# Pooled attention and a gated MLP on one core: float32 probabilities and values in the first two query groups, part of the first weight decode through SBUF, a new order

## The chip, the core and the metric

The kernel runs on one core of a Trainium2 chip. TensorE (PE) multiplies matrices out of SBUF into PSUM. VectorE (DVE), ScalarE (ACT) and GpSimd (POOL) work elementwise; POOL reads and writes SBUF alone. SyncE (SP) issues transfers, and so does ACT in this kernel. Each engine takes its instructions in the order in which the program has them. The metric is the device time of one execution in microseconds; lower is better.

## The reference, cut to what matters

Queries are pooled by two, attended over 1152 keys, and each token's 8 heads of 64 go through a normalized, gated MLP. The weights of the MLP arrive as float64, the rest as float32.

```python
def _attn_ref(q, k, v):                       # 4 batches, 8 heads, 1152 rows, 64 columns
    q_pool = q.reshape(B, H, S // factor, factor, D).mean(axis=3)
    scores = scale * np.matmul(q_pool, k.transpose(0, 1, 3, 2))
    scores = scores - np.max(scores, axis=-1, keepdims=True)
    attn = np.exp(scores)
    attn = attn / (np.sum(attn, axis=-1, keepdims=True) + 1e-09)
    return np.matmul(attn, v).astype(np.float32)

def _moe_ref(x, w_gate, w_val, w_out, rms_g):  # 2304 tokens, 512 wide, 1536 hidden
    rms = np.sqrt(np.mean(x * x, axis=-1, keepdims=True) + 1e-06)
    xn = x / rms * rms_g
    g = xn @ w_gate
    silu = g * (1.0 / (1.0 + np.exp(-g)))
    val = xn @ w_val
    return (silu * val @ w_out).astype(np.float32)
```

## The kernel before

**Precision.** PE multiplies float16 throughout. Where one float16 is too coarse, a float32 value is kept as a high and a low half: `hi_of` (L304 on ACT, L306 on DVE) casts it to float16, `lo_of` (L311, L313) takes what the cast lost. A product of two such values is made of three of the four combinations (`TERMS`); low times low is left out.

**Attention.** Each batch has 576 pooled queries: two full groups of 256 and a rest of 64. A full group has eight strips, one for each head, of 256 queries; the rest has four strips of two heads. In all 12 groups and 80 strips; the first two groups, of batch 0, are strips 1 to 16. For a group, PE first multiplies queries and keys for the row maxima alone (L699), and DVE reduces them (L708), 24 reductions for a full group; the maxima are put into the low half of the queries. Then, for a strip, `emit_scores` (L766) makes the transposed scores with the maximum already taken off, in three PSUM tiles of 768 columns, `emit_exp` (L784) takes the exponential on ACT, `emit_cast` makes the high half of the probabilities (`pT`, L304 or L306), and `emit_lo` the low half: on POOL (L311) if the exponential was put into a scratch tile `p` in SBUF (pool `p32`), on DVE if it was left in PSUM. `emit_pv` (L808) multiplies probabilities and values: for each of two halves of the queries and nine blocks of keys a matmul of the high half with low and high values (130 columns) and one of the low half with the high values (65 columns), 36 in a strip, into the one PSUM bank `o`. `emit_na` (L826) adds the two parts of the result with a reduction on DVE and so frees `o`. The 65th column of the values is a constant, and gives the sum of the probabilities.

**Values and keys.** A head's values are loaded into `st` (ACT queue) and split into high and low halves in one of eight tiles `vv` (L304 or L306, then L313 on DVE). Batch 0's keys are split and turned by PE at the start (L541), those of later batches by a transposing transfer.

**Normalization and MLP.** When a group is done, `add_norm` divides by the sums, normalizes, splits and turns the tokens (`xts`). `add_mlp` multiplies them with gate and value weights (L1011), 48 matmuls of 256 columns to a PSUM tile `ps`, then takes tanh on ACT (L1029), two steps on DVE (L1032, L1035), a cast and a remainder into `hh`, and multiplies with the output weights (L1058).

**Weights.** Float64 words are decoded in 24 jobs of one or two pieces of 512 columns (12 for gate and value, 12 for the output weights): ACT rounds the low words (L390), DVE shifts the high words into a PSUM tile (L395) and joins them (L399), POOL adds both (L405), then cast and remainder as above. All of it is in `add_w`.

**Order.** Every step is an entry in a planner (`Plan`): which engines can do it and for how long by the planner's own tables, what it needs, which buffers it takes and frees, and a rank. `Plan.run` draws up the time line of all engines from that and picks at each point the step that can start first, by rank where there are several. The `T_` constants at the head of the kernel shift the ranks. The program is then written out in that order, and no engine departs from it. PSUM has three tiles `ps` (for maxima, scores, gate and value sums, and the weight decode), `acc` and `o`.

## Time and profile before

| | |
|---|---|
| median of 3 runs | 894.13 us (893.48 to 896.4) |
| span of the profiled execution | 894.0 us (the page gives no other time of it) |
| PE busy | 814.3 us (91%), 8432 matmuls |
| DVE busy | 582.2 us (65%) |
| ACT busy | 528.1 us (59%) |
| POOL busy | 460.3 us (51%) |
| chain that ended last | PE 76%, DVE 10%, ACT 6%, DMA 4% |

The busy time of PE is modelled from pipelined matmuls: a busy PE is not PE at its peak, so the work of a stretch is better read from the count of its matmuls and the spacing of matmuls that run without gaps. The shares are means over stages with different limits. A wait is put down to the step that ended last before it. The granted clock in the table by stretch is that of PE as a share of 2.4 GHz; half of it is 1.2 GHz.

### The profile page before, as it was taken

To read this page: it belongs to the slowest core of one execution; us is meant where nothing else is said; L and a number is where in the kernel's file an instruction comes from. 1 tells how busy PE (TensorE), PEld (TensorE's weight loads), DVE (VectorE), ACT (ScalarE), POOL (GpSimd) and SP (SyncE) were. 2 spreads that over 40 slices of the span, in tenths; PEclk is the share of its full clock that TensorE was granted. 3 is DMA by queue.
4 is the path that set the end of the run, shared out by engine and by line. 5 is a ranking of instruction groups with operands and counts; after the bars stand their busy time and mean duration, and the time that the engine had idled before them with its cause. 6 is when DMAs were issued, how large, how long until landed. Compare 5 with 4: busy or idle time off the path is not lost.

```text
span 894.0 us, 20286 instructions
## 1 busy us (share of the span) xinstructions
PE 814.3 (91%) x8432; PEld 626.6 (70%) x8432; DVE 582.2 (65%) x805; ACT 528.1 (59%) x780; POOL 460.3 (51%) x403
## 2 busy tenths in 40 slices
...
GB/s 315 142 139 143 173 101 163 65 129 184 172 148 86 99 54 94 45 152 162 172 88 51 48 69 63 160 161 118 48 32 69 81 49 34 9 48 1 25 1 24
DMA packets 126956, 87.57 MB, mean 98 GB/s; under 512 B 87184, under 2 KB 105616, under 8 KB 126864
## 3 DMA queue, kind: packets, MB, share of 16 engines
...
## 4 chain that ended last, share of the span: by engine, by line
PE 76%; DVE 10%; ACT 6%; DMA 4%; issue 3%; ACTq 1%; POOL 1%; SPq 0%; POOLq 0%; DVEq 0%
PE ps L1011 30%; PE acc L1058 15%; PE ps L766 14%; PE o L808 11%; PE ps L699 6%; ACT p L784 3%; DVE mx L708 3%; DMA kh<-kT 1%; DVE wg L313 1%; DVE ps L395 1%; DVE vv L313 1%; DMA qT<-q 1%; DMA kT<-kk 1%; DVE wo L399 1%; ACT pT L304 1%
## 5 line engine op out<-in xcount | busy, mean ns | idle before, releaser
L311 POOL TENSOR_TENSOR pT<-p,pT 128x768 f16<-128x768 f32 (+1 forms) x202 | 335.4, 1681 | 123.0 <-DVE pT L306 62.7
L1011 PE MATMUL ps<-xts,wg 128*128 128x256 f16 x2592 | 307.2, 274 | 7.1 <-DVE p L1035 2.9
L1011 PEld LDWEIGHTS <-wg 128*128 128x128 f16 x2592 | 251.7, 98 | 49.4 <-issue 10.8
L708 DVE TENSOR_REDUCE mx<-ps 128x2 f32<-128x768 f32 x216 | 201.3, 953 | 35.0 <-PE ps L699 32.9
L784 ACT ACTIVATE p<-ps,lnp 128x768 f32<-128x768 f32 (+1 forms) x202 | 171.7, 874 | 61.8 <-PE ps L766 50.9
L766 PE MATMUL ps<-qT,kT 128*128 128x256 f16 (+1 forms) x864 | 162.4, 251 | 18.0 <-ACT p L784 12.3
L766 PE MATMUL ps<-qT,kh 65*128 65x256 f16 (+1 forms) x864 | 162.7, 252 | 7.3 <-DMA qT<-q 4.6
L1058 PE MATMUL acc<-wo,hh 128*128 128x512 f16 x648 | 152.5, 379 | 0.8 <-ACT p L1071 0.7
L808 PE MATMUL o<-vv,pT 128*128 128x130 f16 (+2 forms) x2880 | 141.6, 212 | 10.9 <-DVE x L826 6.5
L808 PEld LDWEIGHTS <-pT 128*128 128x128 f16 (+1 forms) x2880 | 132.7, 103 | 24.8 <-POOL pT L311 10.6
L304 ACT ACTIVATE pT<-p 128x768 f16<-128x768 f32 (+1 forms) x167 | 134.8, 824 | 2.7 <-DVE sm L915 0.8
L699 PE MATMUL ps<-kT,qT 128*128 128x384 f16 (+1 forms) x480 | 108.7, 345 | 13.1 <-DVE mx L708 5.5
L1058 PEld LDWEIGHTS <-hh 128*128 128x128 f16 x648 | 62.0, 98 | 65.9 <-issue 2.2
L766 PEld LDWEIGHTS <-kh 65*128 65x128 f16 x864 | 76.7, 100 | 42.0 <-issue 26.8
L766 PEld LDWEIGHTS <-kT 128*128 128x128 f16 x864 | 77.6, 100 | 16.8 <-DVE wo L399 2.5
L1032 DVE SCALAR_TENSOR_TENSOR p<-p,ps 128x512 f32<-128x512 f32 x54 | 36.9, 684 | 77.1 <-ACT p L1029 76.6
L1029 ACT ACTIVATE p<-ps 128x512 f32<-128x512 f32 x54 | 32.2, 596 | 91.2 <-PE ps L1011 91.1
L826 DVE TENSOR_REDUCE x<-o 128x130 f32<-128x260 f32 (+1 forms) x80 | 31.7, 396 | 66.5 <-PE o L808 66.2
L699 PEld LDWEIGHTS <-qT 128*128 128x128 f16 (+1 forms) x480 | 40.8, 104 | 41.1 <-issue 24.1
L304 ACT ACTIVATE hh<-p 128x512 f16<-128x512 f32 x48 | 30.1, 628 | 49.2 <-DVE p L1035 49.2
L405 POOL TENSOR_TENSOR wo<-wo 128x1024 int32<-128x1024 int32 (+1 forms) x20 | 32.2, 1610 | 27.9 <-DVE wo L399 12.4
L1071 ACT ACTIVATE p<-acc 128x512 f32<-128x512 f32 x18 | 10.8, 597 | 56.6 <-PE acc L1058 50.4
...
## 6 DMA issues: line engine op xcount, KB each, us to landing
...
st<-in_v_dram ACTq DMA_DIRECT2D x32, 288.0 KB, 3.5
...
st<-in_k_dram ACTq DMA_DIRECT2D x24, 288.0 KB, 3.3
...
```

What stands on the lines that cost most here:

```text
L304: nc.scalar.activation(out=dst, in_=src, func=AF.Copy, scale=s)
L311: eng.tensor_tensor(out=dst, in0=src, in1=hi, op=ALU.subtract)
L405: nc.gpsimd.tensor_tensor(out=hi, in0=hi, in1=lo, op=ALU.add)
L699: nc.tensor.matmul(out=buf("ps", key)[k * n:(k + 1) * n, a * 512:a * 512 + XP], lhsT=buf("qT", (g["i"], e))[:, 0, hl, c["ci"] * n:(c["ci"] ...
L708: nc.vector.tensor_reduce(out=buf("mx", c["g"]["i"])[:, c["ci"], s:s + 2, p], in_=buf("ps", key).rearrange("p (a c) -> p a c", a=2)[:, :, ...
L766: nc.tensor.matmul(out=sT[:, o:o + n], lhsT=lhsT, rhs=qT[:, 0, hl, :n] if r == 0 else qT[:D + 1, 1, hl, :n], start=(r == 0), stop=(r == 1),)
L784: nc.scalar.activation(out=full(), in_=sT, func=AF.Exp, scale=s_scale, bias=lnp[:, 0:1],)
L808: nc.tensor.matmul(out=o[x * n:(x + 1) * n, c0:], lhsT=pT[:, a, q0:q0 + n], rhs=buf("vv", (u["b"], h))[:, j, c0:OW], start=(j == 0 and a = ...
L1011: nc.tensor.matmul(out=dst, lhsT=wg16[:, e, kb, fg, a, fo:fo + 128], rhs=rhs, start=(i == 0), stop=(i == len(XW) - 1),)
L1029: nc.scalar.activation(out=tv(), in_=gv()[:, :, 0], func=AF.Tanh, scale=0.5 / (X_S * W_S))
L1032: nc.vector.scalar_tensor_tensor(out=tv(), in0=tv(), scalar=1.0, in1=gv()[:, :, 0], op0=ALU.add, op1=ALU.mult)
L1058: nc.tensor.matmul(out=po, lhsT=hh[:, a, f, xo + t0:xo + t0 + 128], rhs=wo16[:, f, r, :], start=(f == fs[0] and a == 0 and r == 0), stop=( ...
```

## The change

In strips 1 to 16 (groups with `whole`) the exponential goes straight from PSUM to SBUF as float32, into the bytes of the two halves of `pT`; the cast and the remainder are gone, and PSUM is free after the exponential. The values of batch 0 are loaded once more, as float32 straight into a `vv` tile, with rows of 65 words (`v_whole`); `emit_pv` then makes 18 float32 matmuls of 65 columns in a strip instead of 36 float16 ones. `emit_na` becomes a copy, on ACT or DVE. The split values of batch 0 are still made, later, for the four strips of its third group, in the same tiles, with eight more small fills on POOL (L623). The scale of the sums follows (`V_ONE`, `g["vs"]`). The first seven weight jobs shift their high words into scratch tiles in SBUF (pool `p32`) instead of PSUM, in pieces of 512 columns. The planner's durations and its `T_` constants are new, and with them the order of all engines.

```diff
--- before.py
+++ after.py
...
+V_ONE = 2.0 ** -7
...
-    T_PE_M = 913.6
+    T_PE_M = 824.5
...
+    T_WHOLE = 0.2
+    T_WM_FROM = 0
+    T_WM_TO = 7
...
+    T_N_WHOLE = 2
+    N_WHOLE = T_N_WHOLE
...
@@ -389,6 +396,24 @@
         lo, _ = w_words(i)
         nc.scalar.activation(out=lo, in_=lo.bitcast(U32), func=AF.Copy, scale=2.0 ** -29)
 
+    def w_tmp(i, e):
+        return buf("p32", ("d", i, e))[:, :WP].bitcast(I32)
+
+    def w_dec_m(i):
+        _, hi = w_words(i)
+        for e in range(w_n[i] // WP):
+            nc.vector.tensor_scalar(
+                out=w_tmp(i, e), in0=hi[:, e], scalar1=3, scalar2=0x3FFFFFF8,
+                op0=ALU.logical_shift_left, op1=ALU.bitwise_and,
+            )
+
+    def w_dec_b(i):
+        _, hi = w_words(i)
+        for e in range(w_n[i] // WP):
+            nc.vector.scalar_tensor_tensor(
+                out=hi[:, e], in0=hi[:, e], scalar=-0x40000000, in1=w_tmp(i, e), op0=ALU.bitwise_and, op1=ALU.bitwise_or
+            )
+
     def w_dec_a(i):
         _, hi = w_words(i)
...
@@ -426,12 +451,17 @@
         if wjobs[i][0] == 2:
             own = [w_done[x] for x in range(i) if w_pools[x] == f"ws{wjobs[i][2]}"]
         if w_is_64:
-            r = add(f"wr{i}", "ACT", 0.25 + 0.833e-3 * n, [d], prio, lambda: w_dec_r(i))
-            a = add(f"wa{i}", "DVE", 0.3 + 2.1e-3 * n, [d], prio, lambda: w_dec_a(i),
-                    alloc=[("ps", ("w", i)), ("pa", ("w", i))], free=[("ps", ("w", i)), ("pa", ("w", i))])
-            s = add(f"ws{i}", "POOL", 0.1 + 2.13e-3 * n, [r, a], prio, lambda: w_dec_s(i))
+            r = add(f"wr{i}", "ACT", 0.19 + 0.928e-3 * n, [d], prio, lambda: w_dec_r(i))
+            if T_WM_FROM <= i < T_WM_TO:
+                tmp = [("p32", ("d", i, e)) for e in range(n // WP)]
+                b = add(f"wm{i}", "DVE", (0.15 + 0.53e-3 * WP) * n / WP, [d], prio, lambda: w_dec_m(i), alloc=tmp, port=True)
+                a = add(f"wa{i}", "DVE", (0.16 + 1.04e-3 * WP) * n / WP, [b], prio, lambda: w_dec_b(i), free=tmp, port=True)
+            else:
+                a = add(f"wa{i}", "DVE", 0.3 + 2.1e-3 * n, [d], prio, lambda: w_dec_a(i),
+                        alloc=[("ps", ("w", i)), ("pa", ("w", i))], free=[("ps", ("w", i)), ("pa", ("w", i))])
+            s = add(f"ws{i}", "POOL", 0.19 + 1.665e-3 * n, [r, a], prio, lambda: w_dec_s(i))
         h = add(f"wh{i}", t_far(n), 0, [s, g_op] + own, prio, lambda: w_hi(i))
-        w_done.append(add(f"wl{i}", {"DVE": 0.45 + 1.04e-3 * n}, 0, [h], prio, lambda: w_lo(i), free=take, port=True))
+        w_done.append(add(f"wl{i}", {"DVE": 0.18 + 1.06e-3 * n}, 0, [h], prio, lambda: w_lo(i), free=take, port=True))
 
 
...
@@ -442,6 +472,8 @@
 
     def add_group(b, i0, n, m):
         g = dict(b=b, i=len(groups), chunks=[], n=n, strips=[])
+        g["whole"] = g["i"] < N_WHOLE and n == 128
+        g["vs"] = 1.0 / V_ONE if g["whole"] else V_S
         groups.append(g)
         for x in range(m):
...
@@ -499,7 +531,11 @@
         nc.scalar.dma_start(out=dst, in_=src[b, h].rearrange("(p c) d -> p c d", c=KC))
 
     kv_op = {}
+    w_op = {}
     k_first = []
+
+    def v_whole(x):
+        return buf("vv", (*x, "w")).rearrange("p c t -> p (c t)").bitcast(F32).rearrange("p (c t) -> p c t", t=XH)
 
     def late_dma():
...
@@ -579,9 +615,16 @@
                               lambda cs=cs: buf("kT", x)[:, cs[0]:cs[-1] + 1], alloc=[] if p else [("kT", x)])
             k_first.append((kl2, ko[0]))
             return
+        if kind == "w":
+            w_op[x] = add(f"vld{x}w", "ACT", 1.3, late_dma() + [v_fill], prio, lambda: ld_kv(x, v, v_whole(x)[:, :, :D]),
+                          alloc=[("vv", (*x, "w"))], lat=0.95, hold=0.45)
+            return
+        zero = v_fill if x[0] or not N_WHOLE else add(f"vz{x}", "POOL", 0.2, [v_fill], prio,
+                   lambda: nc.gpsimd.memset(buf("vv", x)[:, :, D:XH], 0.0), alloc=[("vv", x)])
         vl = add(f"vld{x}", "ACT", 1.1, late_dma(), prio, lambda: ld_kv(x, v, buf("st", ("v", x))), alloc=[("st", ("v", x))], lat=0.95, hold=0.45)
-        vh = add(f"vh{x}", t_hi(KC * D), 0, [vl, v_fill], prio,
-                 lambda: hi_of(buf("vv", x)[:, :, XH:XH + D], buf("st", ("v", x)), V_S), alloc=[("vv", x)])
+        vh = add(f"vh{x}", t_hi(KC * D), 0, [vl, zero], prio,
+                 lambda: hi_of(buf("vv", x)[:, :, XH:XH + D], buf("st", ("v", x)), V_S),
+                 alloc=[("vv", x)] if zero is v_fill else [])
         ko[1] = add(f"vl{x}", {"DVE": 0.25 + 1.04e-3 * KC * D}, 0, [vh], prio,
                     lambda: lo_of(buf("vv", x)[:, :, :D], buf("st", ("v", x)), buf("vv", x)[:, :, XH:XH + D], V_S),
...
@@ -779,6 +822,9 @@
 
 
 
+    def p_whole(u):
+        return buf("pT", u["i"]).rearrange("p a c t -> p (a c t)").bitcast(F32)
+
     def emit_exp(u, js, key, full):
         sT = buf("ps", key)[:, :p_cols(u, js)]
...
@@ -800,6 +846,16 @@
         o = buf("o", u["i"])[:, k * OW:(k + 1) * OW]
         hs = u["heads"]
         n = 128 // len(hs)
+        if u["g"]["whole"]:
+            for j in range(KC):
+                nc.tensor.matmul(
+                    out=o[:, :XH],
+                    lhsT=p_whole(u)[:, j * w + k * 128:j * w + (k + 1) * 128],
+                    rhs=v_whole((u["b"], hs[0]))[:, j],
+                    start=(j == 0),
+                    stop=(j == KC - 1),
+                )
+            return
         for j in range(KC):
             for a in range(2):
...
@@ -822,13 +878,18 @@
         return buf("o", u["i"])[:, :m * OW].rearrange("p (m d) -> p m d", d=OW)
 
     def emit_na(u):
+        if u["g"]["whole"]:
+            hi_of(x_of(u), o_of(u)[:, :, :XH], 1.0)
+            return
         o = o_of(u).rearrange("p m (g c) -> p m c g", g=2)
         nc.vector.tensor_reduce(out=x_of(u), in_=o, op=ALU.add, axis=AX.X)
 
-    k_last, v_last, q_last = {}, {}, {}
...
+                banks = [("ps", key), ("pa", key)]
+                full = lambda j=j: p_whole(u)[:, j[0] * u["w"]:(j[-1] + 1) * u["w"]]
+                e = add(f"E{i}.{t}", "ACT", t_act(n), [s] + ([("after", c0)] if c0 else [x for x, _ in k_first] if i < 2 else []),
+                        R_E + r, lambda j=j, key=key, full=full: emit_exp(u, j, key, full),
+                        alloc=[("pT", i)] if c0 is None else [], free=banks)
+                c0 = c0 or e
+                los.append(e)
+                continue
             e = add(f"E{i}.{t}", "ACT", t_act(n), [s], R_E + r, None)
-            c = add(f"C{i}.{t}", {"ACT": 0.17 + 0.833e-3 * n}, 0, [e] + ([("after", c0)] if c0 else [x for x, _ in k_first] if i < 2 else []), R_L + r,
+            c = add(f"C{i}.{t}", {"ACT": 0.2 + 0.833e-3 * n}, 0, [e] + ([("after", c0)] if c0 else [x for x, _ in k_first] if i < 2 else []), R_L + r,
                     None, alloc=[("pT", i)] if c0 is None else [], port=True)
             c0 = c0 or c
-            lo = add(f"L{i}.{t}", {"DVE": 0.15 + 1.04e-3 * n, "POOL": 0.13 + 2.1e-3 * n}, 0, [c], R_L + r, None)
+            lo = add(f"L{i}.{t}", {"DVE": 0.15 + 1.04e-3 * n, "POOL": 0.18 + 1.914e-3 * n}, 0, [c], R_L + r, None)
...
 
             e.path, e.lo = path, lo
-            prev = s
         m = u["w"] // 128
+        whole = g["whole"]
         for k in range(m):
             last = k == m - 1
-            pv = add(f"V{i}.{k}", "PE", KC * (t_pe(OW) + t_pe(D + 1)) * (1 if len(kvs) == 1 else 1.5),
-                     los + [pv_prev[0]] + [kv_op[x][1] for x in kvs], PE_V + r, lambda k=k: emit_pv(u, k),
+            pv = add(f"V{i}.{k}", "PE", KC * T_WHOLE if whole else KC * (t_pe(OW) + t_pe(D + 1)) * (1 if len(kvs) == 1 else 1.5),
+                     los + [pv_prev[0]] + [w_op[x] if whole else kv_op[x][1] for x in kvs], PE_V + r, lambda k=k: emit_pv(u, k),
                      alloc=[("o", i)] if k == 0 else [],
-                     free=([("pT", i)] + [("vv", x) for x in kvs if k_last[x] == i]) if last else [])
+                     free=([("pT", i)] + ([("vv", (*x, "w")) for x in kvs if x_whole[x] == i] if whole
+                                          else [("vv", x) for x in kvs if k_last[x] == i])) if last else [])
             pv_prev[0] = ("after", pv)
         lead = [("after", g["strips"][0]["x"])] if u["slot"] else q_first if g["i"] < 2 else []
-        u["x"] = add(f"na.{i}", "DVE", 0.15 + 2.08e-3 * m * XH, [pv] + lead, R_N + r, lambda: emit_na(u),
+        way = {"DVE": 0.15 + 2.08e-3 * m * XH}
+        if whole:
+            way = {"ACT": 0.25 + 0.833e-3 * m * XH, "DVE": 0.15 + 1.04e-3 * m * XH}
+        u["x"] = add(f"na.{i}", way, 0, [pv] + lead, T_R_NW + r if whole else R_N + r, lambda: emit_na(u),
                      alloc=[("x", g["i"])] if u["slot"] == 0 else [], free=[("o", i)])
...
@@ -1113,8 +1188,7 @@
 
     def fill_v():
         for x in bufs["vv"]:
-            nc.gpsimd.memset(x[:, :, D:XH], 0.0)
-            nc.gpsimd.memset(x[:, :, XH + D:], 1.0)
+            nc.gpsimd.memset(x.rearrange("p c t -> p (c t)").bitcast(F32).rearrange("p (c t) -> p c t", t=XH)[:, :, D:], V_ONE)
 
...
@@ -1125,13 +1199,17 @@
     kh_fill = add("fk", "POOL", 0.6, [], -9e5, fill_k)
     v_fill = add("fv", "POOL", 0.6, [], -8e5, fill_v)
     g_op = add("g", "SP", 0.1, [], -5.0, g_load, lat=2.0, hold=0.45)
-    jobs = []
+    jobs, split = [], set()
     seen = set()
     for u in strips:
         for h in u["heads"]:
             if (u["b"], h) not in seen:
                 seen.add((u["b"], h))
                 jobs.append((u["r"] - K_AHEAD - (0 if u["b"] else T_K0), 1, "k", (u["b"], h)))
+                if u["g"]["whole"]:
+                    jobs.append((u["r"] - V_AHEAD, 2, "w", (u["b"], h)))
+            if not u["g"]["whole"] and (u["b"], h) not in split:
+                split.add((u["b"], h))
                 jobs.append((u["r"] - V_AHEAD, 2, "v", (u["b"], h)))
     for g in groups:
         for c in g["chunks"]:
```

Three places in the new order. First PE in the first strips, where a strip's product of probabilities and values begins behind scores of the next (`kT`, `kh` are keys, `vv` values, `pT` probabilities, `ps` and `o` PSUM tiles). Before:

```order
L766 LDWEIGHTS kh_74
L766 MATMUL ps_99<-qT_86,kh_74 128x256
L808 LDWEIGHTS pT_93
L808 MATMUL o<-vv_75,pT_93 128x130
L808 LDWEIGHTS pT_93
L808 MATMUL o<-vv_75,pT_93 128x65
```

and now:

```order
L809 LDWEIGHTS kh_74
L809 MATMUL ps_101<-qT_87,kh_74 128x256
L851 MATMUL o<-vv_75,pT_93 128x65 x9
L809 LDWEIGHTS kT_66
L809 MATMUL ps_100<-qT_87,kT_66 128x256
```

A pair of loads and a pair of matmuls, nine times over for each half of the queries, has become nine float32 matmuls; their weight loads are no instructions of their own in the program.

Second ACT at strips 1 and 2 (`p` is scratch, `mx` the maxima, `wo` and `wg` weights, `x` the result of attention, `lnp` a constant). Before:

```order
L784 ACTIVATE p_90<-ps_99,lnp 128x768
L304 ACTIVATE pT_94<-p_90 128x768
L390 ACTIVATE wo_105<-wo_105 128x512
L784 ACTIVATE p_91<-ps_99,lnp 128x768
L304 ACTIVATE pT_94<-p_91 128x768
L390 ACTIVATE wo_105<-wo_105 128x512
L784 ACTIVATE p_92<-ps_101,lnp 128x768
L304 ACTIVATE pT_94<-p_92 128x768
L784 ACTIVATE p_88<-ps_99,lnp 128x768
L304 ACTIVATE p_89<-mx_95 128x4
L304 ACTIVATE pT_93<-p_88 128x768
L304 ACTIVATE wg_104<-wo_105,g_sb 128x2x512
```

and now:

```order
L311 ACTIVATE q_84<-qst_83 128x512
L830 ACTIVATE pT_93<-ps_101,lnp 128x768
L830 ACTIVATE pT_93<-ps_99,lnp 128x768
L830 ACTIVATE pT_93<-ps_101,lnp 128x768
L397 ACTIVATE wo_105<-wo_105 128x512
L830 ACTIVATE pT_94<-ps_99,lnp 128x768
L397 ACTIVATE wo_105<-wo_105 128x512
L311 ACTIVATE wg_104<-wo_105,g_sb 128x2x512
L830 ACTIVATE pT_94<-ps_101,lnp 128x768
L830 ACTIVATE pT_94<-ps_100,lnp 128x768
L311 ACTIVATE wo_105<-wo_105 128x512
L311 ACTIVATE x_97<-o 128x2x65
```

Each exponential had a cast behind it; now three exponentials follow each other with weight steps between the strips, and the result's copy is in this queue. On POOL, where 43 rows into the program the remainders of `pT` began, the first one now stands 74 rows in, behind strip 16; before it stand the adds of the weight decode.

Third DVE ahead of the first row maximum (`vv` values, `wo` the staged words and `wg` gate and value weights, `kT` keys). Before:

```order
L313 SCALAR_TENSOR_TENSOR vv_75<-st_61,vv_75 128x9x64
L313 SCALAR_TENSOR_TENSOR vv_76<-st_62,vv_76 128x9x64
L395 TENSOR_SCALAR ps_100<-wo_105 128x1024
L399 SCALAR_TENSOR_TENSOR wo_105<-wo_105,ps_100 128x1024
L395 TENSOR_SCALAR ps_101<-wo_105 128x1024
L399 SCALAR_TENSOR_TENSOR wo_105<-wo_105,ps_101 128x1024
L708 TENSOR_REDUCE mx_95<-ps_99 128x2
L708 TENSOR_REDUCE mx_95<-ps_101 128x2
L313 SCALAR_TENSOR_TENSOR vv_77<-st_61,vv_77 128x9x64
```

and now:

```order
L413 SCALAR_TENSOR_TENSOR wo_105<-wo_105,p_90 128x512
L413 SCALAR_TENSOR_TENSOR wo_105<-wo_105,p_91 128x512
L313 TENSOR_SCALAR kT_72<-ps_101 128x768
L313 TENSOR_SCALAR wg_104<-wo_105,g_sb 128x2x512
L405 TENSOR_SCALAR p_92<-wo_105 128x512
L405 TENSOR_SCALAR p_90<-wo_105 128x512
L320 SCALAR_TENSOR_TENSOR wg_104<-wo_105,g_sb,wg_104 128x2x512
L413 SCALAR_TENSOR_TENSOR wo_105<-wo_105,p_92 128x512
L413 SCALAR_TENSOR_TENSOR wo_105<-wo_105,p_90 128x512
L751 TENSOR_REDUCE mx_95<-ps_101 128x2
L751 TENSOR_REDUCE mx_95<-ps_99 128x2
L751 TENSOR_REDUCE mx_95<-ps_100 128x2
```

The remainders of the values have gone from here; the first maximum stands behind the whole decode of the first weight job, its cast and its remainder, with the second job's first steps between them.

## Rows read from the trace of the kernel before

**Rows 1.** The page: the span of the profiled execution, and its instructions.

```profile
span 894.0 us, 20286 instructions
```

**Rows 2.** By stretch: length; PE, PEld, DVE, ACT, POOL busy; PEclk, DMA, GB/s.

```profile
0.00:56.00 56.00, 33.25 (x210) 20.57 (x210) 48.46 (x63) 39.90 (x60) 24.68 (x45) 1.00 0.66 219
56.00:126.00 70.00, 52.47 (x556) 40.22 (x554) 60.69 (x73) 61.11 (x80) 60.66 (x38) 0.88 0.43 122
126.00:181.00 55.00, 41.50 (x414) 33.85 (x411) 41.86 (x39) 38.62 (x50) 34.77 (x26) 0.75 0.46 126
181.00:300.00 119.00, 108.14 (x1164) 84.56 (x1163) 100.03 (x143) 73.22 (x118) 64.59 (x59) 0.99 0.63 145
300.00:782.00 482.00, 471.50 (x5318) 371.09 (x5318) 303.06 (x451) 294.13 (x439) 273.97 (x231) 1.00 0.37 84
```

**Rows 3.** PE matmuls by line, 0 to 181 us: busy, mean ns, idle before.

```profile
L766 PE MATMUL ps<-qT,kh 65*128 65x256 f16 x144 | 39.8, 306 | 3.4 <-DMA qT<-q 3.4
L766 PE MATMUL ps<-qT,kT 128*128 128x256 f16 x144 | 39.6, 304 | 12.0 <-ACT p L784 8.0 <-DVE pT L311 2.0 <-DVE wo L399 1.4
L808 PE MATMUL o<-vv,pT 128*128 128x130 f16 x576 | 37.5, 230 | 9.8 <-DVE x L826 6.0 <-POOL pT L311 3.7
L699 PE MATMUL ps<-kT,qT 128*128 128x384 f16 (+1 forms) x120 | 31.6, 394 | 7.8 <-DVE mx L708 3.0 <-ACT p L784 2.9 <-DVE wo L399 1.4
L1011 PE MATMUL ps<-xts,wg 128*128 128x256 f16 x84 | 11.8, 293 | 2.3 <-ACT p L784 2.3
```

**Rows 4.** The chain of waits in time: start us, length us, what.

```profile
170.34 1.59 PE o L808 x36
...
282.59 1.34 PE ps L766 x12
...
308.76 1.31 PE ps L1011 x12
...
344.57 1.30 PE acc L1058 x6
```

**Rows 5.** The page's costliest groups: counts; for weight loads their mean.

```profile
L1011 PE MATMUL ps<-xts,wg 128*128 128x256 f16 x2592 | 307.2, 274 | 7.1 <-DVE p L1035 2.9
...
L1058 PE MATMUL acc<-wo,hh 128*128 128x512 f16 x648 | 152.5, 379 | 0.8 <-ACT p L1071 0.7
...
L766 PE MATMUL ps<-qT,kh 65*128 65x256 f16 (+1 forms) x864 | 162.7, 252 | 7.3 <-DMA qT<-q 4.6
...
L808 PEld LDWEIGHTS <-pT 128*128 128x128 f16 (+1 forms) x2880 | 132.7, 103 | 24.8 <-POOL pT L311 10.6
...
L699 PE MATMUL ps<-kT,qT 128*128 128x384 f16 (+1 forms) x480 | 108.7, 345 | 13.1 <-DVE mx L708 5.5
```

**Rows 6.** DVE by line, 0 to 125.6 us.

```profile
L708 DVE TENSOR_REDUCE mx<-ps 128x2 f32<-128x768 f32 x48 | 44.3, 951 | 4.8 <-PE ps L699 4.4
...
L313 DVE SCALAR_TENSOR_TENSOR vv<-st,vv 128x576 f16<-128x576 f32 x8 | 9.5, 1205 | 0.0
L313 DVE SCALAR_TENSOR_TENSOR wg<-wo,g_sb,wg 128x1024 f16<-128x1024 f32 x6 | 9.1, 1516 | 4.1 <-ACT wg L304 4.1
...
L826 DVE TENSOR_REDUCE x<-o 128x130 f32<-128x260 f32 x10 | 4.2, 418 | 0.0
...
L311 DVE TENSOR_TENSOR pT<-ps,pT 128x768 f16<-128x768 f32 x3 | 2.8, 942 | 0.0
```

**Rows 7.** POOL and ACT by line, 56 to 181 us: remainders and casts.

```profile
L311 POOL TENSOR_TENSOR pT<-p,pT 128x768 f16<-128x768 f32 x37 | 66.8, 1826 | 2.7 <-ACT pT L304 1.3 <-POOL pT L311 1.0 <-PE ps L766 0.4
...
L304 ACT ACTIVATE pT<-p 128x768 f16<-128x768 f32 x37 | 30.7, 840 | 1.4 <-DVE sm L915 0.8
```

**Rows 8.** The page's DMA issues: count, KB each, median us to landing.

```profile
st<-in_v_dram ACTq DMA_DIRECT2D x32, 288.0 KB, 3.5
```

**Rows 9.** DVE by line and shape, whole span.

```profile
L395 DVE TENSOR_SCALAR ps<-wo 128x512 int32<-128x512 int32 x8 | 5.5, 686 | 0.0
```

70 lines of the change are left out of this document (38 added, 32 removed).

## The prediction

> **What bounds the kernel now.** I read the span first [rows 1]: 894.0 us. Nothing else of that execution's time is given; the median of the runs is 894.13 us, so some 0.1 us lies around the span. Then the table by stretch [rows 2]: from 300 us on TensorE (PE) is busy 471.5 of 482 us, before that it is not. To say how much it loses I price its work at the spacing seen where it runs without gaps [rows 4]: 36 products of probabilities and values in 1.59 us (44 ns each), 12 score matmuls in 1.34 us (112 ns), 12 gate/value matmuls in 1.31 us (109 ns), 6 output matmuls in 1.30 us (217 ns). A 384-column matmul of the row maxima I take by its columns, 163 ns, the 576 narrow scores at 30 ns, a 128-column turn at 58 ns (estimates). With the counts [rows 5] (2880 products; of 1728 scores 1152 are wide): gate/value 283, output 140, scores 129 + 17, maxima 78, products 127, 104 turns 6. Sum 780 us. So 894 - 780 = 114 us are lost on PE.
>
> Where: up to 181 us [rows 3] PE has done 576 products (16 strips of 36), 288 scores, 120 maxima, 84 gate/value matmuls and 104 turns: 25 + 32 + 20 + 9 + 6 = 92 us of work. So 89 of the 114 us are lost in the first 181, and 25 in the 713 that follow. In the first 56 us it has 210 matmuls [rows 2], 48 maxima, 30 scores, 32 products and 100 turns: 18 us, and it loses 38. Between 56 and 181 it loses the other 51. There VectorE (DVE), ScalarE (ACT) and GpSimd (POOL) are all busy about 61 of 70 us, and still 42, 39 and 35 of 55 [rows 2]; PE is held in turn by ACT, DVE and POOL [rows 3], and its granted clock has a mean of 0.88 and then 0.75, so part of it runs at 1.2 GHz of 2.4. This stretch, strips 1 to 16, is the one that the change rebuilds.
>
> **The change part by part.** (1) *Taken from ACT and POOL.* Each of the 16 strips loses three casts and three remainders. Between 56 and 181 us these are 37 casts of 0.84 us on ACT and 37 remainders of 1.83 us on POOL [rows 7], and a few more each outside this view. Of POOL's 95.4 us in that stretch [rows 2] 66.8 go. ACT takes over 14 of the 16 copies of the product's result (DVE reduces them today in 0.42 us each [rows 6]), about 5 us, and is still some 30 us lighter. From then on neither sets the pace of strips 1 to 16.
>
> (2) *DVE is not relieved before the 48th maximum.* That reduction ends at 125.5 us; 48 of them, 44.3 us, are the largest part of DVE's 109 us up to there [rows 2, 6]. In the new order the 48th again stands near the same place in the queue (132nd row; before, 128th). Gone ahead of it: eight value remainders (9.5 us), ten reductions of results (4.2 us) and three remainders of probabilities (2.8 us) [rows 6], 17 us in all. Come in: three more gate/value remainders at 1.5 us [rows 6], 4.5 us; four weight casts that ACT did, the first group's normalization and two more casts of k, some 7 us by their sizes (an estimate); and the weight decode of 13 instead of 12 jobs, of which the first seven go through SBUF in 512-wide pieces. The first step of such a piece is no row of before: at 0.69 us, as through PSUM [rows 9], the extra job, two pieces of two steps, costs 2.8 us; at two thirds of that, if SBUF is read faster, the eleven pieces save 2.5 us and it is paid. Together about 12. So DVE has about 104 us of work there, and with the 17 us of idle time it has today [rows 2] the 48th maximum ends near 120 us. The first maximum now waits behind one whole weight decode; I put 2 us of that on the first strip (40 us lost instead of 38).
>
> (3) *Put on PE.* 576 products go: 16 x 1.59 = 25.4 us. 288 float32 matmuls with 128-column weights and 65 moving columns come. No row shows a float32 matmul. From below: 0.088 us, the pair of matmuls that it replaces (nothing gained or lost; a float32 operand carries the bytes of both halves, so a gain is excluded). From above: four weight loads at their whole duration of 0.103 us [rows 5], 0.412 us. Between: the pair multiplies three of the four combinations of high and low halves, at 44 ns a matmul with its load [rows 4]; a float32 product keeps all four, 4 x 0.044 = 0.18 us, and its four loads no longer hide behind a 130-column matmul. I take 0.2 us, nearest to that: 57.6 us, so PE's work becomes 780 - 25.4 + 57.6 = 812 us.
>
> The Trainium skill (FP8 and Floating Point Precision, TensorE Precision Notes) has true FP32 as four passes through the array; no run here shows it. At 44 ns a pass it would give 0.176 us a product and 876 us in all.
>
> (4) *The start with these terms.* When the 96th matmul of the maxima issues, PE has 104 turns, 198 scores and 180 float32 products behind it: 6 + 16 + 22 + 36 = 80 us, and with 40 lost it is there at 120, just when DVE is. Up to strip 16's product follow 90 scores, 108 float32 products, 4 maxima and 18 gate/value matmuls: 10 + 22 + 1 + 2 = 34 us. In this part PE should run nearly alone: one strip holds PE for 12 x 3 x 0.112 + 18 x 0.2 = 7.6 us and ACT for three exponentials, each about as long as a cast. Each product must still wait until the strip before has been copied out of the one result bank, now by a copy in ACT's queue behind exponentials and weight steps; today this wait is 6.0 us [rows 3], and I keep 6 us. Strip 16 ends near 160 us instead of 181, with 114 us of work done: 46 us lost instead of 89.
>
> (5) *Put elsewhere.* Eight more loads of values, 288 KB each, in 256-byte pieces (their rows are 65 words apart). A load of values lands in 3.5 us today [rows 8], in pieces of 2304 bytes; nine times as many pieces, at worst nine times as long, 32 us. Taken at twice, 7 us: the first is issued on ACT behind the copies of the seventh head's keys, some 30 us ahead of its product, so nothing lies on the path; at the worst price the product of a strip would come a few us late. Nothing behind strip 16 loses work on PE; the 25 us lost there I keep. The first hidden-layer step on DVE now stands behind six maxima and an extra normalization, but PE may issue 144 gate/value matmuls (three PSUM buffers of 48, 16 us) before it needs that step.
>
> The sum: 812 + 46 + 25 = 883 us; as a balance, 894 + 32 (work) - 43 (loss) = 883.
>
> **The rivals.** *Dear products.* If the float32 loads cannot be hidden, PE is the bound from the first strip: every 0.01 us more costs 288 x 0.01 = 2.9 us, without cover, since DVE is already met at 120. It decides from 0.24 us on: 883 + 288 x 0.04 = 894; at 0.412 us the time is 883 + 288 x 0.212 = 944. For it: in today's products load and matmul alternate within 44 ns although a load lasts 103 ns [rows 4, 5], so their speed rests on hidden loads. Against: so little of the matmul's time is needed to hide them that four half-products at that pace are 0.18 us.
>
> The Trainium skill (TensorE: Matmul & The Clock Gate, Weight-path perf modes) says that the fast weight load is on only for weights that are not FP32. No trace here shows it either way; it is this rival's mechanism. The same page's estimate of a load, 128 columns / 1.2, is 107 ns; four of them make 0.43 us and 949 us in all.
>
> *Cheap products.* At 0.12 us PE would be ahead of DVE at the 48th maximum, which stays at 120; then 13 + 13 + 6 us to strip 16 at 152, with 91 us of work done and 61 lost. 789 + 61 + 25 = 875 us; at 0.088 us it is 871. Here DVE is the floor: cheaper products bring little.
>
> *The gain is given back.* DVE is busy 100 of 119 us between 181 and 300 [rows 2]. If the stage that follows strip 16 can't come forward with it, because weights, the third group's maxima and the first hidden-layer steps queue on DVE, some 10 us of the 43 are lost again and the time is 893 us. For: the work up to the 60th maximum is within a few us the same in both orders. Against: PE's own work from strip 16 to strip 21 is some 96 us, longer than what DVE has queued there.
>
> **How the numbers follow.** The forecast, a price of 0.17 to 0.23 us and 874 to 891 us, has 0.45. Dear products have 0.28 (891 to 944; 0.06 of it within 0.3% of today, 0.22 slower). Cheap ones have 0.17 (870 to 875). Given back: 0.10, of which 0.06 is within 0.3% and 0.04 slower. A measurement of this kernel tells about 0.3%, 2.7 us, from no change. So faster 0.45 + 0.17 = 0.62, same 0.12, slower 0.26. Range: 868 holds all but a little of the cheap case; above, a price up to 0.28 us gives 906, which leaves out about 0.15 of the dear one. Predicted: 883 us, 868 to 906.
>
> **What would show it.** In the changed profile: no remainders on POOL in the first 160 us; the 48th maximum still at 115 to 125 us; one float32 product (18 matmuls) every 3.6 us where PE runs without gaps; the 16th strip's product at about 160 us; PE without long gaps from 120 us on. The forecast is wrong if 18 products take over 4.4 us (dear) or under 2.5 (cheap), if the 48th maximum comes after 130 us (then DVE's queue was lengthened, not kept), or if the loss behind strip 16 is well above 25 us.

## The result, and the profile after

The changed kernel takes 884.23 us (median of four), the kernel before 894.14 us beside it on the same chip: a ratio of 0.9868, 95% interval 0.983 to 0.9906, so faster by 0.9 to 1.7%. One of the four executions, at 901.51 us, ran in a slower state of the chip with a lower granted clock, and the ratio leaves it out, as all ratios here do with such executions. The forecast was 883 us, in a range of 868 to 906. The profiled execution took 881.1 us, the fastest of the four, with a span of 879.1 us, so 2.0 us lie around the span, not 0.1. In later executions of before it is 1.8 us (898.05 us with a span of 896.3); the profiled one of before, whose own time was not given, must then have taken about 896 us (an estimate).

The page and the table by stretch of the changed kernel, against [rows 1] and [rows 2]; columns as there (length; PE, PEld, DVE, ACT, POOL busy; PEclk, DMA, GB/s):

```profile
span 879.1 us, 20165 instructions
```

```profile
0.00:56.00 56.00, 34.09 (x218) 23.61 (x218) 43.57 (x66) 34.08 (x51) 15.45 (x30) 0.91 0.80 234
56.00:126.00 70.00, 65.88 (x557) 57.83 (x555) 56.59 (x70) 44.86 (x64) 20.65 (x23) 1.00 0.53 150
126.00:181.00 55.00, 53.07 (x497) 47.21 (x496) 46.54 (x59) 34.03 (x52) 18.03 (x23) 1.00 0.59 169
181.00:300.00 119.00, 115.59 (x1289) 92.44 (x1288) 100.57 (x143) 76.56 (x117) 73.70 (x57) 1.00 0.60 137
300.00:782.00 482.00, 469.99 (x5176) 363.74 (x5175) 328.39 (x472) 270.75 (x405) 259.54 (x212) 0.99 0.37 82
```

From 56 to 181 us PE is now busy 119 of 125 us (94 before), and its granted clock is 1.00 all through (0.88 and 0.75 before). POOL has 39 us of work there for 95. The timeline of POOL shows the first remainder of probabilities (start, length):

```profile
182.16 2.96 POOL L318 TENSOR_TENSOR pT<-p,pT 128x768 f16<-128x768 f32 x2 [1.10 <-ACT pT L311]
```

In the chain of waits a group of float32 products shows as 18 records; each product is two weight loads and two matmuls:

```profile
69.83 1.34 PE ps L809 x12
71.17 1.96 PE o L851 x18
```

So 18 records are nine products, half of a strip, in 1.96 us: 0.218 us a product, 109 ns a record. All 576 records are 62.7 us. (The prediction counted 18 products to 3.6 us; they take 3.92.) By the prediction's prices, not rounded, PE's work is 781 us before (780 in the prediction) and 818 us now.

PE's matmuls by line up to the end of strip 16 (busy, mean ns, idle time before them and who ended it), against [rows 3]:

```profile
L851 PE MATMUL o<-vv,pT 128*128 128x65 f32 x576 | 68.0, 273 | 0.8 <-ACT x L311 0.7
L809 PE MATMUL ps<-qT,kT 128*128 128x256 f16 x144 | 35.1, 278 | 4.4 <-ACT pT L830 4.1 <-DVE wo L424 0.2
L809 PE MATMUL ps<-qT,kh 65*128 65x256 f16 x144 | 35.0, 278 | 0.6 <-DMA qT<-q 0.3 <-DMA kh<-kT 0.3
L742 PE MATMUL ps<-kT,qT 128*128 128x384 f16 (+1 forms) x108 | 26.9, 365 | 3.6 <-DVE mx L751 2.0 <-ACT qT L311 1.4
```

The waits ahead of scores, products and maxima are 9.4 us in all; before they were 33 us [rows 3]. That is 24 us. The rest of what PE gained here is its clock. The stretch up to the end of strip 16 in one row, before and then changed (columns as in the table):

```profile
0.00:180.60 180.60, 126.82 (x1170) 94.55 (x1172) 150.60 (x172) 139.63 (x188) 120.10 (x108) 0.88 0.51 154
```

```profile
0.00:163.60 163.60, 135.64 (x1088) 114.95 (x1090) 130.01 (x168) 103.07 (x148) 46.53 (x64) 0.97 0.66 188
```

PE is idle 54 us before and 28 now, 26 us less. A mean clock of 0.88 over 180.6 us is 43 us at 1.2 GHz, one of 0.97 over 163.6 us is 10; 33 us less at half the speed are worth up to 17 us. 26 + 17 is about the 44.6 us by which the loss up to strip 16 fell.

### The profile page after: what moved, and what is told of

The parts are those of the page before. It is cut to its first block, busy times and chain, and to the rows that moved or that the text cites. A ratio compares the mean times of both kernels' runs of the same rounds, so it can differ in the third digit from the quotient of the medians.

```text
span 879.1 us, 20165 instructions
## 1 busy us (share of the span) xinstructions
PE 831.2 (95%) x8432; PEld 653.7 (74%) x8432; DVE 600.5 (68%) x842; ACT 477.8 (54%) x714; POOL 387.4 (44%) x344
## 4 chain that ended last, share of the span: by engine, by line
PE 80%; DVE 6%; ACT 4%; issue 4%; DMA 3%; POOL 2%; ACTq 1%; SPq 0%; DVEq 0%; POOLq 0%
PE ps L1086 29%; PE ps L809 14%; PE acc L1133 14%; PE o L864 9%; PE o L851 7%; PE ps L742 6%; DVE mx L751 3%; ACT p L830 2%; POOL pT L318 1%; DMA kh<-kT 1%; DMA wo<-in_moe_w_val_dram 1%; DVE hh L318 1%; DVE p L1110 1%; DVE p L1107 1%; ACT pT L830 1%
## 5 line engine op out<-in xcount | busy, mean ns | idle before, releaser
L318 POOL TENSOR_TENSOR pT<-p,pT 128x768 f16<-128x768 f32 (+1 forms) x168 | 274.4, 1656 | 132.1 <-DVE pT L313 84.1
L830 ACT ACTIVATE p<-ps,lnp 128x768 f32<-128x768 f32 (+1 forms) x168 | 141.9, 867 | 58.0 <-PE ps L809 49.0
L809 PE MATMUL ps<-qT,kT 128*128 128x256 f16 (+1 forms) x864 | 158.9, 247 | 9.9 <-ACT pT L830 4.1
L809 PE MATMUL ps<-qT,kh 65*128 65x256 f16 (+1 forms) x864 | 159.0, 248 | 1.1 <-DMA kh<-kT 0.8
L864 PEld LDWEIGHTS <-pT 128*128 128x128 f16 (+1 forms) x2304 | 98.2, 101 | 10.9 <-issue 4.6
L864 PE MATMUL o<-vv,pT 128*128 128x130 f16 (+3 forms) x2304 | 105.1, 207 | 0.0
L311 ACT ACTIVATE pT<-p 128x768 f16<-128x768 f32 (+1 forms) x128 | 100.5, 805 | 1.6 <-PE o L864 0.3
L851 PEld LDWEIGHTS o<-vv,pT 128*128 128x128 f32 x576 | 67.0, 192 | 2.4 <-ACT x L311 1.4
L851 PE MATMUL o<-vv,pT 128*128 128x65 f32 x576 | 68.0, 273 | 0.8 <-ACT x L311 0.7
L885 DVE TENSOR_REDUCE x<-o 128x130 f32<-128x260 f32 (+1 forms) x64 | 25.0, 391 | 40.7 <-PE o L864 40.4
```

The costliest lines, as they stand in the source:

```text
L311: nc.scalar.activation(out=dst, in_=src, func=AF.Copy, scale=s)
L318: eng.tensor_tensor(out=dst, in0=src, in1=hi, op=ALU.subtract)
L809: nc.tensor.matmul(out=sT[:, o:o + n], lhsT=lhsT, rhs=qT[:, 0, hl, :n] if r == 0 else qT[:D + 1, 1, hl, :n], start=(r == 0), stop=(r == 1),)
L830: nc.scalar.activation(out=full(), in_=sT, func=AF.Exp, scale=s_scale, bias=lnp[:, 0:1],)
L851: nc.tensor.matmul(out=o[:, :XH], lhsT=p_whole(u)[:, j * w + k * 128:j * w + (k + 1) * 128], rhs=v_whole((u["b"], hs[0]))[:, j], start=(j ...
L864: nc.tensor.matmul(out=o[x * n:(x + 1) * n, c0:], lhsT=pT[:, a, q0:q0 + n], rhs=buf("vv", (u["b"], h))[:, j, c0:OW], start=(j == 0 and a = ...
```

## The experiments

Medians of before differ a little from chip to chip (894 to 898 us), so kernels of different runs are compared by their ratios. The columns on strips and losses come from one profiled execution of each kernel and are sure to some 3 us: strip 1, which the edits of experiment 2 leave as it is, ends at 56.4 us in the profile of before and at 59.2 and 59.1 in theirs, with a granted clock of 0.86 for 1.00 up to 56 us. They are read in the same way for all: the end of a strip is the end of its last product, and the loss is the time gone less the work done by then at the prediction's prices (a float32 record at 109 ns). The "order" is what the planner makes of the kernel's table of numbers; "its own" is the order of the named kernel, kept instruction for instruction.

| kernel | ratio to before (95%) | order | loss by strip 1 | strip 16 ends | loss by strip 16 | loss after it |
|---|---|---|---|---|---|---|
| before | 1 | own | 38 | 180.6 | 89 | 24 |
| changed | 0.9868 (0.983 to 0.9906) | own | 35 | 163.6 | 44 | 17 |
| order only | 1.0144 (1.0119 to 1.0168) | new | 44 | 190.2 | 102 | 27 |
| float32 only | 1.0128 (1.0101 to 1.0154) | new | 42 | 172.8 | 52 | 33 |
| no decode in SBUF | 1.0124 (1.0102 to 1.0146) | new | 42 | 177.3 | 55 | 30 |
| one group | 1.0084 (1.0053 to 1.0114) | new | 37 | 178.3 | 67 | 35 |
| one number changed | 1.0199 (1.0105 to 1.0293) | new | 35 | 178.3 | 59 | 29 |
| before, short remainders | 0.9894 (0.986 to 0.9927) | before's | 41 | 175.0 | 83 | 24 |
| ... and short casts | 0.983 (0.9785 to 0.9874) | before's | 41 | 166.9 | 75 | 23 |
| changed, 5 of 9 products | 0.9786 (0.9757 to 0.9815) | changed's | 35 | 157.8 | 66 | 17 |
| fitted, no float32, no SBUF | 0.9996 (0.997 to 1.0021) | fitted | 35 | 177.0 | 75 | 37 |
| fitted, no SBUF | 1.0052 (1.0032 to 1.0071) | fitted | 38 | 170.9 | 53 | 25 |
| fitted, all parts | 0.9847 (0.9822 to 0.9873) | fitted | 36 | 164.6 | 45 | 19 |

**1. One part undone, or done alone.** Four kernels: no float32 strips; float32 strips alone in the kernel before; every decode through PSUM; float32 in the first group alone.

```diff
# order only
-    T_N_WHOLE = 2
+    T_N_WHOLE = 0
...
+            nc.gpsimd.memset(x[:, :, D:XH], 0.0)
# float32 only: all T_ numbers and planner prices of the kernel before
-    T_WM_TO = 7
+    T_WM_TO = 0
...
# no decode in SBUF
-    T_WM_TO = 7
+    T_WM_TO = 0
# one group
-    T_N_WHOLE = 2
+    T_N_WHOLE = 1
```

Order only. 

> The changed kernel with no float32 strips: probabilities and values of all groups are split into two halves again, while the new order, the new prices of the planner and the decode through SBUF stay. Theory T (the casts and remainders that leave ACT and POOL in strips 1 to 16 pay for the dearer products): TensorE's work falls by 62.7 - 25.4 = 37 us, to about 782 us, and its loss rises again to about that of the kernel before, 105 to 115 us, so 887 to 897 us. Rival O (the new order and prices bring the gain, float32 is neutral or costs): the loss stays near the 61 us of the changed kernel, 845 to 870 us, or at least under 880.

Float32 only. 

> The kernel before with the float32 strips alone: old order numbers, old planner prices, every decode through PSUM. T: most of the gain is there, strip 16 at 162 to 170 us, 883 to 890 us. Rival O: the 37 us of dearer products are not paid back under the old order, 900 to 930 us. Rival D (the decode through SBUF frees PSUM and is what shortens the start): 890 to 897 us.

No decode in SBUF. 

> The changed kernel with the first seven decode steps through PSUM, as in the kernel before; everything else stays. T: the decode is neither bound nor cover, 881 to 888 us. Rival D: the gain falls away, 890 to 896 us.

One group. 

> The changed kernel with float32 in the first query group alone (8 strips for 16). T: half of the dearer products (about 19 us less work for TensorE, 800 us) and remainders and casts back in strips 9 to 16, where the maxima still run until 125 us: 884 to 892 us. Rival O: half the price is saved and nothing is lost, 862 to 872 us.

Measured: 909.64, 907.56, 907.12 and 902.22 us, before 895.66 us. All four are slower than both kernels. For float32 alone rival O had said so (900 to 930); the other three lie where no theory put them. In these orders neither float32 nor the new numbers are a gain alone, and half of the float32 part is not half of the gain. Float32 alone did lower the loss by strip 16 from 89 to 52 us (strip 16 at 172.8 us; T had 162 to 170), but its dearer products cost the same 37 us, and the loss behind strip 16 grew from 24 to 33 us. Without float32 the clock between 56 and 181 us is lower than the changed kernel's 1.00; the table by stretch of the order alone:

```profile
56.00:126.00 70.00, 50.89 (x488) 38.49 (x489) 59.14 (x72) 51.27 (x70) 44.94 (x31) 0.79 0.56 148
126.00:181.00 55.00, 34.84 (x393) 28.69 (x391) 44.35 (x44) 42.63 (x56) 39.25 (x29) 0.78 0.42 119
```

Against the changed kernel each of the four costs 19 to 25 us (by the ratios), even the one without the decode in SBUF, which is a few us of DVE's work. But in all four the planner lays out every engine anew, with numbers that were not chosen for that work.

**2. The relief, by itself.** To leave the order alone, the kernel before was kept instruction for instruction and only the sizes were cut, from the third strip on.

```diff
     def emit_cast(u, js, full):
-        hi_of(p_part(u, js, 0), full(), 1.0)
+        c = 32 if 2 <= u["i"] < 16 else p_cols(u, js); hi_of(p_part(u, js, 0)[:, :c], full()[:, :c], 1.0)
     def emit_lo(u, js, full):
-        lo_of(p_part(u, js, 1), full(), p_part(u, js, 0), 1.0)
+        c = 32 if 2 <= u["i"] < 16 else p_cols(u, js); lo_of(p_part(u, js, 1)[:, :c], full()[:, :c], p_part(u, js, 0)[:, :c], 1.0)
```

Remainders alone (the second half of the edit). 

> The kernel before in its own order, on every engine, with the remainders of strips 3 to 16 cut to 32 of up to 768 columns (the rest of the lower half is left as the strips before wrote it, so the output isn't the reference's). Float32 alone and order alone were each slower than before, so this takes the relief by itself: nothing is put in another place and no product is dearer. T (the remainder on POOL, and the wait for it, is most of what TensorE loses until strip 16): the loss by strip 16 falls from 89 to 50 to 65 us, 862 to 880 us. Rival W (the casts and the maxima set the pace, the remainder only lies behind them): the loss stays above 80 us, 886 to 895 us.

Remainders and casts. 

> As the kernel before it, with the casts of the same strips cut to 32 columns too: what float32 takes off ACT and POOL, without its dearer products. T: the loss by strip 16 falls to about the 52 us of the float32 strips under the old order, 850 to 865 us; 37 us of dearer products then eat this up, which is why float32 alone gained nothing. Rival W (maxima and decode on DVE set the pace): 880 to 895 us, and the loss by strip 16 stays above 75 us.

Measured: 887.21 and 880.95 us, before 898.05 us. These are rival W's numbers, not T's: the loss by strip 16 is 83 and 75 us, 6 and 14 us less than before (8 and 16 if counted from strip 1). With casts and remainders all but gone for nothing in return, the kernel before gains 1.1 and 1.7%, about 10 and 15 us. Of the 43 us by which the prediction let this loss fall, part is the dearer products themselves, which fill waits of PE: at 0.088 us a product, as dear as today's, its own working gives 871 us, that is 780 + 66 + 25, a loss lower by 23 us. So in the old order the relief is worth 14 to 16 us of those 23. What still holds PE there, by line up to strip 16:

```profile
L766 PE MATMUL ps<-qT,kT 128*128 128x256 f16 x144 | 38.2, 296 | 13.3 <-ACT p L784 9.4 <-DVE wo L399 2.5 <-DVE pT L311 0.6
L808 PE MATMUL o<-vv,pT 128*128 128x130 f16 x576 | 35.1, 224 | 1.6 <-DVE x L826 1.6
L699 PE MATMUL ps<-kT,qT 128*128 128x384 f16 (+1 forms) x118 | 31.0, 394 | 5.9 <-DVE mx L708 2.8 <-ACT p L784 1.4 <-DMA qT<-q 1.2
```

The wait of the products is down to 1.6 us (9.8 in [rows 3]), that of the scores for an exponential is not (9.4 us; 8.0 before): in this order the exponentials come late with or without the casts beside them. So it is not the maxima alone that hold PE (2.8 us of waits), as W had it; which instruction ahead of the exponentials does, wasn't tried.

**3. What the products' price does.** The changed kernel in its own order, with the row chunks 1, 3, 5 and 7 left out of the float32 sums:

```diff
-            for j in range(KC):
+            for j in range(0, KC, 2):
```

> The changed kernel in its own order with five of the nine float32 products of each strip half left out of the sum (the row chunks with odd numbers), so the output isn't the reference's. TensorE's work falls by 16 x 2 x 4 x 0.218 = 27.9 us. If TensorE is the bound all through strips 1 to 16 (T as forecast, with dear products as the price): 856 to 862 us. If the maxima on DVE hold strips 1 to 10 (they end at 126.6 us with these products): those ten strips give nothing back and the other six 16 x ... = 6 x 1.74 = 10.5 us, so 870 to 876 us, strip 10 still at about 123 us.

(The text leaves out four of nine products; "five" there is a slip, its 27.9 us are four.) Measured: 877.83 us, before 898.05 us: 7.3 us less than the changed kernel by the ratios, of 27.9 us of work. This is the price of the prediction's cheap rival, 5/9 of 0.218 = 0.121 us for a product, and it gave 875 us; 0.9786 x 894.14 is 875.0. The total agrees by luck: the rival had strip 16 at 152 us with 61 lost and 25 lost behind it, measured are 157.8, 66 and 17, and the two errors cancel. The second reading of the expectation (870 to 876 us) has the total too, but not the path: strip 10 ends at 116.4 us, not 123, and the six strips behind it give nothing more back. The maxima (DVE by line; window up to 121 us here, to 126.7 us in the changed kernel; the second row is the latter):

```profile
L751 DVE TENSOR_REDUCE mx<-ps 128x2 f32<-128x768 f32 x48 | 43.9, 951 | 9.7 <-PE ps L742 8.3 <-ACT wg L311 1.4
```

```profile
L751 DVE TENSOR_REDUCE mx<-ps 128x2 f32<-128x768 f32 x48 | 44.5, 954 | 12.9 <-PE ps L742 12.7
```

With cheap products the 48th maximum ends at 120.9 us, where the prediction had it, though DVE waits 8.3 us for PE there too; with the real ones at 126.6, DVE having waited 12.7 us for PE (4.4 before [rows 6]). But strip 16 comes only 5.8 us sooner: the loss by then rises from 44 to 66 us. The table by stretch says why (56 to 181 us, then all up to the end of strip 16):

```profile
56.00:126.00 70.00, 59.29 (x445) 47.77 (x444) 59.90 (x73) 46.89 (x67) 22.54 (x25) 0.90 0.61 167
126.00:181.00 55.00, 49.30 (x384) 38.85 (x384) 47.13 (x59) 34.30 (x52) 19.11 (x24) 0.84 0.57 156
```

```profile
0.00:157.80 157.80, 121.53 (x832) 93.15 (x834) 129.56 (x168) 102.94 (x147) 46.53 (x64) 0.91 0.70 195
```

PE is idle 36 us up to strip 16 (28 in the changed kernel), and the clock from 56 us on, 1.00 in the changed kernel, is down to 0.90 and 0.84: 14 + 18 = 32 us at 1.2 GHz. Up to strip 16 the mean is 0.91 for 0.97, 28 us at 1.2 GHz for 10, which is up to 9 us of loss. The lower clock is no accident of one profile: over whole executions it is 0.967 to 0.980 in the four of this kernel, 0.979 to 0.990 in the three of the changed kernel that its ratio counts. The pages' rows in 40 slices of 22 us (busy tenths of PE; granted clock in tenths), first of this kernel, then of the changed one:

```profile
PE   4699779999999999999998999999999999999997
...
PEclk9999697999999999999999999999999999999999
```

```profile
PE   4599899999999999999998999999999999999997
...
PEclk9899999999999999999999999999999999999999
```

PE is held up in the fifth and sixth slice (0.7 busy), and the clock falls in the fifth and seventh. Part of what a shorter product saves is so paid back, in waits and at half speed.

**4. What sets the price.** The changed kernel in its own order; strips 2 to 8 multiply 33 of 65 value columns, strips 9 to 16 load 64 of 128 probability columns.

```diff
+            cols = 33 if 1 <= u["i"] < 8 else XH
+            rows = 64 if u["i"] >= 8 else 128
...
-                    out=o[:, :XH],
+                    out=o[:rows, :cols],
```

> The changed kernel in its own order; strips 2 to 8 multiply only the first 33 of 65 value columns, strips 9 to 16 load only 64 of 128 probability columns as weights, so the output isn't the reference's. What is read is the time of 18 records where TensorE runs without gaps, 1.96 us in the changed kernel (109 ns a record). If the moving columns set it: about 1.0 us in strips 2 to 8, 1.96 in strips 9 to 16. If the weight load sets it: 1.96 us in strips 2 to 8, about 1.0 in strips 9 to 16. If a fixed time for each record: 1.96 in both. By the first, 882 us at most; by the second 880 us, by the third 884.

Measured: 882.25 us, a single execution, which tells nothing between 880, 882 and 884; the records do. In the chain of waits, 18 records in strips 2 to 8, and in strips 9 to 16:

```profile
84.89 1.93 PE o L853 x18
...
148.62 1.19 PE o L853 x18
```

Half the moving columns change next to nothing (107 ns a record for 109), half the weight columns make it 66 ns, 0.61 of the time and not the half that was expected (1.19 us, not 1.0). So at 128 weight columns a product's price is its weights, two loads' worth, and the 65 moving columns are hidden behind them; what makes up the 66 ns at 64 columns wasn't tried. The Trainium skill (TensorE: Matmul & The Clock Gate, LDWEIGHTS) estimates a load by its columns alone, 107 ns for 128 of them; the trace agrees if a float32 product has two such loads, one to each record of 109 ns. For 64 columns the same estimate is 53 ns, and a record takes 66.

**5. The order alone.** One number of the planner's changed, no instruction added or taken away:

```diff
-    T_WHOLE = 0.2
+    T_WHOLE = 0.22
```

> The changed kernel with one number of the planner changed: the price it holds for a float32 product, 0.20 to 0.22 us, which is nearer to the measured 0.218. No instruction is added or taken away; the order of all engines comes out differently. T (the parts of the change count, whatever the exact order): 881 to 888 us. Rival L (the recorded order is one that happens to be good, and another order of the same work loses 10 us or more, so that every undone part loses that as well): 893 to 910 us.

Measured: 921.59 us (median of four; the ratio rests on two, 907.98 and 921.16), before 898.05 us: a price nearer to the truth made the same work 2 to 4% slower than the changed kernel (by the ratios). The profiled execution is the one of 907.98 us. Until strip 1 the two are alike, then this order leaves PE without work; 56 to 181 us:

```profile
56.00:126.00 70.00, 62.70 (x515) 54.69 (x515) 51.93 (x65) 40.03 (x56) 17.11 (x18) 0.95 0.53 143
126.00:181.00 55.00, 46.48 (x387) 40.83 (x387) 42.95 (x56) 31.47 (x47) 14.44 (x19) 0.91 0.70 174
```

Rival L holds, and its 893 to 910 us were low rather than high: this order alone costs more than the whole change brings, and experiment 1 had mixed parts and order up.

**6. Each variant with an order of its own.** For three variants the table of numbers was therefore searched anew, by the planner's own total, which it computes ahead of any run (23 numbers each; the lowest total found was taken).

```diff
# fitted, no float32, no decode in SBUF (all numbers new)
-    T_PE_V = 13.5
+    T_PE_V = 148.71
...
-    T_WM_TO = 7
+    T_WM_TO = 0
...
-    T_N_WHOLE = 2
+    T_N_WHOLE = 0
...
# fitted, no decode in SBUF
-    T_PE_V = 13.5
+    T_PE_V = 231.22
...
-    T_WHOLE = 0.2
+    T_WHOLE = 0.218
...
-    T_WM_TO = 7
+    T_WM_TO = 0
...
# fitted, all parts
-    T_PE_V = 13.5
+    T_PE_V = 169.6
...
```

No float32. 

> The changed kernel without float32 strips and without the decode through SBUF, so with the work of the kernel before, but under an order of its own: the planner's numbers were searched for this very work, by the planner's own total, until that fell from 924 to 900 us (the changed kernel's own total is 890.5, that of the kernel before 908.8 under its older prices; the planner is a few us off, 6 too high for the changed kernel). Theory F (with an order fitted to each, float32 is worth some 10 us): 888 to 898 us, about the kernel before. Rival L (the fitting alone is the gain, the parts are not needed): 884 us or less.

No decode in SBUF. 

> The changed kernel with every decode through PSUM, this time under an order searched for it, with the measured price of 0.218 us for a float32 product: the planner's own total is 897.3 us, where the same search gave 893.9 with the decode through SBUF. Theory F with a small part for the decode: 884 to 893 us, and the 23 us that its removal cost under the old numbers were the unfitted order. Rival D (the decode through SBUF itself carries the gain): 898 to 908 us, as without the fitting.

All parts. 

> The changed kernel with all its parts, under another order that the same search found from its own numbers (the planner's total 887.4 us for 890.5). It tells whether the recorded order can be replaced, and is the candidate to beat both kernels. Theory F (the parts carry the gain, any fitted order will do): 878 to 887 us. Rival L (the recorded order was picked by what the chip does with it, and one that only the planner likes better loses): 890 to 910 us.

Measured: 895.12, 899.76 and 881.49 us, before 895.5 us. The work of the kernel before under a fitted order is where it was (0.9996): this other order by itself brings nothing, as F said. All the parts under another fitted order are as fast as the changed kernel (0.9847 against 0.9868, intervals that overlap): the recorded order is not unique. It is faster than the kernel before; that it beats the changed one isn't shown. Float32 without the decode in SBUF missed F's numbers and fell into rival D's: 0.5% slower than before, and some 18 us slower than with all parts. Its planner also had 0.218 us for a float32 product, the other one 0.2; a number like this moved experiment 5, and the two weren't told apart. (The decode in SBUF without float32 was run only in the unfitted order of experiment 1, so that the decode alone carries the gain isn't shown either.) Where PE waits up to strip 16 in that kernel, by line, against the rows of the changed kernel above:

```profile
L809 PE MATMUL ps<-qT,kT 128*128 128x256 f16 x144 | 36.1, 284 | 5.2 <-ACT pT L830 3.3 <-DVE wo L424 1.3 <-ACT qT L311 0.4
L742 PE MATMUL ps<-kT,qT 128*128 128x384 f16 (+1 forms) x100 | 28.2, 397 | 10.4 <-ACT qT L311 3.3 <-DMA qT<-q 2.8 <-DVE wo L424 2.1
```

PE waits 3.4 us for the decode's second step (DVE wo L424) to give a PSUM bank back; 0.2 us in the changed kernel. And the decode waits for its banks: DVE's first step, whole span, in this kernel, then in the changed one:

```profile
L420 DVE TENSOR_SCALAR ps<-wo 128x1024 int32<-128x1024 int32 x12 | 14.7, 1222 | 7.0 <-ACT pT L830 3.7 <-DMA wo<-in_moe_w_val_dram 3.3
```

```profile
L420 DVE TENSOR_SCALAR ps<-wo 128x1024 int32<-128x1024 int32 x8 | 9.8, 1224 | 3.7 <-DMA wo<-in_moe_w_val_dram 2.8 <-ACT pT L830 0.9
```

So PSUM banks are part of what the decode in SBUF frees, some 6 us of waits on two engines, which can overlap. The clock differs as well; the stretch up to strip 16 in this kernel:

```profile
0.00:170.90 170.90, 138.49 (x1078) 116.75 (x1080) 131.91 (x160) 103.24 (x147) 47.49 (x65) 0.90 0.64 182
```

Here PE is idle 32 us, 4 more than in the changed kernel, and 34 us run at 1.2 GHz for 10, up to 12 us of loss. The two kernels are 9 us apart by strip 16 and 8 us more behind it; how much of that is the bank, how much the clock and how much one order against another isn't settled by one order each.

## Why the prediction came out, point by point

The time was met (883 for 884), the balance less well: 883 = 812 + 46 + 25 was forecast, 818 + 44 + 17 = 879 of span was found, with 2 us around it. That the sum comes out to 1 us is luck: work was 6 us too low, loss behind strip 16 was 8 us too high, and the profiled execution is the fastest.

1. *Taken from ACT and POOL*: the work went much as said; 95 us of POOL's are 39. What the relief is worth was too high: of the 43 us of loss, 23 are relief alone by the prediction's own working, and in the old order 14 to 16 were measured (experiment 2). The other part, that dearer products fill PE's waits, held: in the changed order the loss is 66 us with cheap products and 44 with the real ones. It fell to 44 us only where relief, the decode out of PSUM and an order fitted to both came together, and not by waits alone (26 us less idle, up to 17 us by the clock), where the prediction named the clock and gave it no term.
2. *DVE up to the 48th maximum*: near 120 us was forecast, of 104 us of work and 17 of idle time. It ends at 120.9 us where products are cheap, but of 100 and 21 us, with 8.3 us of waiting for PE, so that this is DVE's floor isn't shown. In the changed kernel it ends at 126.6 us, outside the 115 to 125 that should have shown the prediction right, since PE, not DVE, is late with the maxima there. The decode's first step in SBUF takes 0.46 us, two thirds of 0.69, the better end of its bounds:

```profile
L405 DVE TENSOR_SCALAR p<-wo 128x512 int32<-128x512 int32 x11 | 4.9, 464 | 1.5 <-DMA wo<-in_moe_w_val_dram 1.1 <-DMA wo<-in_moe_w_out_dram 0.3 <-DMA wo<-in_moe_w_gate_dram 0.2
L413 DVE SCALAR_TENSOR_TENSOR wo<-wo,p 128x512 int32<-128x512 int32 x11 | 7.5, 712 | 0.0
```

   Counting the decode in DVE's time alone was the step that failed: without it float32 gained nothing in either order tried, while DVE's work up to the 48th maximum was 103 us for 101. PSUM banks are part of it; the rest stays open (experiment 6).
3. *The product*: 0.218 us for 0.2, inside the forecast's 0.17 to 0.23, +5 us. The reason was wrong: not four half-products at 44 ns but two records of 109 with a weight load each.
4. *Strip 16*: 163.6 us for 160, 44 us lost for 46; 5 us more of products, 2 us less of loss. The wait for the result bank, kept at 6 us, is 0.7.
5. *Behind strip 16*: 17 us lost, 25 had been kept. Here an error of 8 us hid that of the price. The table shows what this loss goes with: 24, 24 and 23 us in the three kernels in the order of before, 17 and 17 us in two in the changed order (19 in the third, experiment 4), 19 to 37 in the others. It goes with the order, not with what the strips do.

Of the rivals, dear products fell (0.218, and it decided from 0.24). The cheap rival was not the case; when the price was lowered its total came out, but of two parts that were each off (experiment 3). That the gain is given back behind strip 16 did not happen in this order; in others it did (29 to 35 us lost there in the four unfitted orders with float32, 24 before), and the prediction's reason against it (PE's own work is longer than DVE's queue) doesn't tell one order from another, so this rival was undervalued. That the order in itself could decide, by 2 to 4% with no instruction added or taken away, was no rival at all, and should have been.
